# A decode block on one core: the same work, written with waits by hand and a hardware loop for TensorE

## The chip, the core and the metric

The kernel runs on one core of one Trainium2 chip. The metric is the device time of one execution in microseconds. A core has TensorE (PE, with its weight loads listed as PEld), VectorE (DVE), ScalarE (ACT), GpSimd (POOL) and SyncE (SP, which here only issues DMAs), and 16 DMA engines that carry its transfers.

## The reference

Four tokens (B = 4, one position each) go through an attention block over a cache and an MLP, and the results are summed:

```python
x = A_x                                    # (4, 1, 512)
xn = layernorm(x)
q = (xn @ wq) -> (4, 32 heads, 1, 128)
scores = q . k_cache * 128 ** -0.5         # k_cache (4, 32, 4096, 128)
o = softmax(scores) . v_cache              # v_cache (4, 32, 4096, 128)
out = x + o @ wo + B_ref(xn)
# B_ref on one position: xn + gelu(layernorm(xn) @ w3) @ w4, w3 (512, 1792), w4 (1792, 512)
```

All numbers are float32. With one position, the shifts of the mixing step of `B_ref` take only padding, so w1 and w2 have no effect. Both caches are 268 MB each and each byte of them is used once.

## The kernel before, in words

The 128 pairs of batch and head are worked through in 32 groups of four heads (`NJ = 32`, `G = 4`). A group has 8.39 MB of K and as much of V, each as one tile of 128 partitions with 64 KB in a row; 32 partitions belong to a head, and a partition holds 128 positions (`R = 128`).

The scores are not made by TensorE. VectorE multiplies the K tile, in place, by the query, repeated over all partitions of its head and all positions (L219), and sums over the 128 numbers of each position (L220). Then it finds the maximum of each head (L222 to L226: maximum in a partition, a transpose, maximum over the 32). ScalarE takes the exponentials, one head at a time, into `pw`, and keeps their sums in `rs` (L235). TensorE multiplies the weights with V, 32 products a group (L244; each appears as two matmuls and two weight loads in a trace).

The kernel is written in a language with a scheduler: tiles come from pools (`ks` has two buffers for K, `vs` one for V), and the waits follow from what each instruction reads and writes. `tc.issue_after` holds some work back.

Every second group (`y` counts pairs of groups), TensorE's result `pv` is copied by ScalarE (`os`, L250), summed over the partitions of each head by TensorE (`oz`, L253, with the sums of the weights, L255), and divided by VectorE (L257, L260). After eight groups, one batch, `spread` brings the result into the layout `X` that the last product needs (L263 to L266). Every fourth group, `queries` has TensorE spread the queries of four groups over all partitions, into PSUM (`qb`, L209). POOL clears the half of `pw` that the next group doesn't fill (L231).

All large loads are issued by SP, in one order: w3, wq, K(0), K(1), V(0), K(2), V(1), and so on. SP waits for the buffer of the next load to come free: K(j+2) waits for the sums of K(j) (L220), V(j+1) for the products of V(j) (L244). At the end the second buffer of K takes V(31), then w4 goes where V was, and wo follows in five pieces, when the last K tile has been summed (L322).

Before the groups stand two layernorms, the first half of the MLP (L176 to L187) and the queries (`pq`, L198). Behind them stand the second half of the MLP (L284), the product with wo (L331 into `y`, L326 into `total`), a copy (L341) and four small stores (L344).

Of the kernel before, what the change touches and what calls it, by code (L numbers as in the profile page):

```python
# [41 lines left out]
G = 4  # L42


@with_exitstack
def decode_block(ctx: ExitStack, tc: tile.TileContext, x, k, v, wq, wo, w3, w4, out):
# [12 lines left out]
    WC = H * DH // P  # L59

    consts = ctx.enter_context(tc.tile_pool(name="consts", bufs=1))
    ks = ctx.enter_context(tc.tile_pool(name="ks", bufs=2))
    vs = ctx.enter_context(tc.tile_pool(name="vs", bufs=1))
    work = ctx.enter_context(tc.tile_pool(name="work", bufs=2))
    psum = ctx.enter_context(tc.tile_pool(name="psum", bufs=2, space=PSUM))
# [4 lines left out]
    def slot(pool, name):  # L70
        return pool.tile([P, R * DH], F32, tag="rows", name=name)

    def group_rows(flat, j):
        n = G * S * DH
        return flat[j * n:(j + 1) * n].rearrange("(p c d) -> p c d", p=P, c=R)


    w3_slot = slot(vs, "w3")
    w3_sb = w3_slot[:, :NC * F].rearrange("p (c f) -> p c f", c=NC)
    spare = w3_slot[:, NC * F:]  # L80
    xs = spare[:B, :D]
    nc.scalar.dma_start(xs, x.rearrange("b s d -> (b s) d"))
    nc.sync.dma_start(w3_sb, w3.rearrange("(p c) f -> p c f", c=NC))  # L83
    wq_sb = slot(ks, "wq").rearrange("p (c n) -> p c n", c=NC)
    nc.sync.dma_start(wq_sb, wq.rearrange("(p c) n -> p c n", c=NC))  # L85

    K, V = {}, {}

    def load_k(j):
        K[j] = slot(ks, f"k{j}").rearrange("p (c d) -> p c d", c=R)  # L90
        nc.sync.dma_start(K[j], group_rows(kf, j))

    def load_v(j, pool=vs):
        V[j] = slot(pool, f"v{j}").rearrange("p (c d) -> p c d", c=R)
        nc.sync.dma_start(V[j], group_rows(vf, j))

    load_k(0)


    ident = consts.tile([P, P], F32, name="ident")  # L100
    make_identity(nc, ident)
    ones = consts.tile([P, 1], F32, name="ones")
    nc.vector.memset(ones, 1.0)
    eps = consts.tile([B, 1], F32, name="eps")
    nc.vector.memset(eps, EPS)

    sel = consts.tile([P, HP], F32, name="sel")
    nc.vector.reduce_sum(sel, ident.rearrange("p (q m) -> p m q", q=G), axis=AX.X)
    mask = consts.tile([P, G], F32, name="mask")
    nc.vector.reduce_sum(mask, ident.rearrange("p (q m) -> p q m", q=G), axis=AX.X)  # L110

    selb = consts.tile([P, B, G, HP], F32, name="selb")
    for b in range(B):
        nc.vector.tensor_copy(selb[:, b], ident.rearrange("p (q m) -> p q m", q=G)[:, :, b:b + 1].to_broadcast([P, G, HP]))

    pw = consts.tile([P, NG, 32], F32, name="pw")
    os = consts.tile([P, 4, DH], F32, name="os")
    RS = []
    for n in range(2):
        rs = consts.tile([P, 2, G], F32, name=f"rs{n}")  # L120
        nc.gpsimd.memset(rs, 0.0)
        RS.append(rs)
    lt = consts.tile([P, H, 4], F32, name="lt")

    X = consts.tile([P, WC, B], F32, name="X")


    lnc = spare[:B, D:2 * D]
    lnq = os.rearrange("p m d -> p (m d)")[:B, :]

    def layernorm(src, o, name):
        s = work.tile([B, 4], F32, tag="lns", name=f"{name}s")
        nc.vector.reduce_sum(s[:, 0:1], src, axis=AX.X)
        nc.vector.tensor_scalar_mul(s[:, 0:1], s[:, 0:1], 1.0 / D)
        nc.vector.tensor_scalar(lnc, src, s[:, 0:1], None, op0=ALU.subtract)
        nc.vector.tensor_mul(lnq, lnc, lnc)
        nc.vector.reduce_sum(s[:, 1:2], lnq, axis=AX.X)
        nc.scalar.activation(s[:, 2:3], s[:, 1:2], AF.Sqrt, bias=eps, scale=1.0 / D)
        nc.vector.reciprocal(s[:, 3:4], s[:, 2:3])
        nc.vector.tensor_scalar_mul(o, lnc, s[:, 3:4])  # L140

    def transposed(src, o, name):

        nc.gpsimd.memset(o, 0.0)
        pt = psum.tile([P, NC, B], F32, tag="b", name=f"{name}p")
        for c in range(NC):
            nc.tensor.matmul(pt[:, c, :], src.rearrange("b (p c) -> b c p", c=NC)[:, c, :], ident[:B, :B],
                             start=True, stop=True)
        nc.vector.tensor_copy(o[:, :, 0:B], pt)  # L149

    pw_row = pw.rearrange("p g m -> p (g m)")
    xn = pw_row[:B, 0:D]
    x1n = pw_row[:B, D:2 * D]
    layernorm(xs, xn, "xn")
    xnT = X.rearrange("p c b -> p (c b)").rearrange("p (c m) -> p c m", c=NC)
    transposed(xn, xnT, "xnT")
    layernorm(xn, x1n, "x1n")
    x1nT = lt.rearrange("p h q -> p (h q)").rearrange("p (c m) -> p c m", c=NC)
    transposed(x1n, x1nT, "x1nT")


    total = psum.tile([P, P], F32, tag="total", bufs=1, name="total")
    for t in range(4):
        for n, src in enumerate((xs, xn)):
            nc.tensor.matmul(total[32 * t:32 * t + 32, :], ident[:B, 0:32], src[:, P * t:P * t + P],
                             start=(n == 0), stop=False)
    nc.gpsimd.memset(pw, 0.0)


    gT = consts.tile([P, NF, B], F32, name="gT")  # L170

    def mlp_up():
        ph = psum.tile([P, FT], F32, tag="qb", name="ph")
        for c in range(NC):
            for t in range(4):
                nc.tensor.matmul(ph[32 * t:32 * t + 32, :], x1nT[:, c, :], w3_sb[:, c, t * FT:(t + 1) * FT],  # L176
                                 start=(c == 0), stop=(c == NC - 1))
        hs, u, t, gt = (w3_slot[:, n * FT:(n + 1) * FT] for n in range(4))
        nc.scalar.copy(hs.rearrange("p (m i) -> p m i", i=32), ph.rearrange("p (i m) -> p m i", i=32))  # L179
        nc.vector.tensor_mul(u, hs, hs)  # L180
        nc.vector.tensor_scalar(u, u, GELU_B, 1.0, op0=ALU.mult, op1=ALU.add)
        nc.vector.tensor_mul(u, u, hs)
        nc.scalar.activation(t, u, AF.Tanh, scale=GELU_A)
        nc.vector.tensor_scalar(t, t, 1.0, 0.5, op0=ALU.add, op1=ALU.mult)
        nc.vector.tensor_mul(hs, hs, t)
        nc.vector.transpose(gt, hs)
        nc.vector.tensor_copy(gT, gt.rearrange("p (m i) -> p m i", i=32)[:, :, 0:B])  # L187

    mlp_up()


    q_sb = consts.tile([P, 2, 4 * DH], F32, name="q_sb")
    pq = [psum.tile([P, 4 * DH], F32, tag="pv", name=f"pq{n}") for n in range(2)]
    wq_h = wq_sb.rearrange("p c (n j h d) -> p c n h j d", n=2, j=4, h=G)
    for c in range(NC):
        for n in range(2):
            for h in range(G):
                nc.tensor.matmul(pq[n][HP * h:HP * h + HP, :], xnT[:, c, :], wq_h[:, c, n, h],  # L198
                                 start=(c == 0), stop=(c == NC - 1))
    for n in range(2):  # L200
        nc.scalar.mul(q_sb[:, n, :], pq[n], DH ** -0.5)


    QBC, SC, NM, DONE, PVS, OT, SUMMED = {}, {}, {}, {}, {}, {}, {}

    def queries(y):
        b, n = divmod(y, 2)
        QBC[y] = psum.tile([P, 4, DH], F32, tag="qb", name=f"qb{y}")
        nc.tensor.matmul(QBC[y], selb[:, b], q_sb[:, n, :], start=True, stop=True)  # L209

    def scores(j):

        with tc.issue_after(DONE[j - 1]) if j > 0 else nullcontext():
            scores_of(j)

    def scores_of(j):
        SC[j] = work.tile([P, R], F32, tag="sc", name=f"sc{j}")
        q = QBC[j // 4][:, j % 4, :].unsqueeze(1).to_broadcast([P, R, DH])
        nc.vector.tensor_tensor(out=K[j], in0=K[j], in1=q, op=ALU.mult)  # L219
        nc.vector.reduce_sum(SC[j], K[j], axis=AX.X)  # L220
        rm = work.tile([P, 1], F32, tag="rm", name=f"rm{j}")
        nc.vector.reduce_max(rm, SC[j], axis=AX.X)  # L222
        tr = work.tile([P, HP], F32, tag="tr", name=f"tr{j}")
        nc.vector.transpose(tr, rm.to_broadcast([P, HP]))  # L224
        NM[j] = work.tile([P, 1], F32, tag="nm", name=f"nm{j}")
        DONE[j] = nc.vector.tensor_reduce(NM[j], tr, axis=AX.X, op=ALU.max, negate=True).ins  # L226

    def weights(j):
        y, r = divmod(j, 2)
        rs = RS[y % 2]  # L230
        nc.gpsimd.memset(pw[:, :, 16 * (1 - r):16 * (1 - r) + 16], 0.0)  # L231
        for h in range(G):
            s = slice(HP * h, HP * h + HP)
# [4 lines left out]
    def values(j):  # L238
        y, r = divmod(j, 2)
        if r == 0:  # L240
            PVS[y] = psum.tile([P, 4 * DH], F32, tag="pv", name=f"pv{y}")
# [49 lines left out]
    for j in range(NJ):  # L291
# [8 lines left out]
        if j + 2 < NJ:  # L300
            load_k(j + 2)
# [71 lines left out]
```

## Time and profile before

| | us |
|---|---|
| median of three runs | 1308.79 (1308.0 to 1309.28) |
| the profiled execution | 1309.46 |
| its span in the profile | 1307.7 |
| busy: VectorE | 1141.0 (87%) |
| busy: TensorE, weight loads | 356.8, 115.9 |
| busy: ScalarE, POOL | 79.0, 19.1 |
| data moved | 561.38 MB, 429 GB/s over the span |
| instructions in the trace | 5929, of them 2508 matmuls and 2508 weight loads |

The page of the profile lists busy times, DMA queues, the chain that ended last and groups of instructions. A row of a group or of a timeline has the line in the kernel, the engine, the operation, the tile written and the tile read, sizes, and in brackets or behind the bar the idle time ahead of it and what ended that. In a timeline the first two numbers are the start and the length in microseconds from the start of the span. In the list of queues, q1 is SP's, q10 ScalarE's, and the queues named "instruction" carry the engines' own code. A row of windows gives the stretch and its length, each engine's busy time with its count, the granted clock of TensorE, the mean busy share of the 16 DMA engines, and GB/s.

### The profile page before, as it was taken

The page shows a single profiled execution, that of the slowest core. Times are in us where ns is not written, and L with a number is a line of the kernel's source. Part 1 is how long each engine was busy: PE and PEld are TensorE (multiplying, and loading weights), DVE is VectorE, ACT ScalarE, POOL GpSimd, SP SyncE. Part 2 cuts the span into 40 slices and gives each one's busy share as a digit, 9 for nine tenths or more (in the row PEclk, how much of TensorE's full clock was granted, in tenths as well). Part 3 has the DMA queues.
Part 4 walks back from the last instruction along what each step waited for, and adds up shares of the span by engine and source line. Part 5 has one row for each costly group of instructions (what it writes and reads, how often), then busy time and mean ns, then how long its engine had stood idle before and what let it go on. Part 6 is the DMA issues. An engine that isn't in the chain of part 4 may idle for free.

```text
span 1307.7 us, 5929 instructions
## 1 busy us (share of the span) xinstructions
PE 356.8 (27%) x2508; PEld 115.9 (9%) x2508; DVE 1141.0 (87%) x228; ACT 79.0 (6%) x285; POOL 19.1 (1%) x45
## 2 busy tenths in 40 slices
PE   3220323221232321123232033322123332112337
PEld 1000101000010100001010010100001010000102
DVE  3499999998898998888899888898889899888880
ACT  1000000000000000000000000000000000000000
POOL 0000000000000000000000000000000000000000
PEclk8655666656666665666665566665666666566668
DMA  9999999999999999999999999999999999999997
GB/s 403 446 419 439 427 441 425 441 426 439 429 435 432 435 429 435 435 432 435 432 432 439 431 436 429 436 431 434 431 435 436 427 440 427 439 427 438 429 424 317
DMA packets 10434, 561.38 MB, mean 429 GB/s; under 512 B 1172, under 2 KB 1188, under 8 KB 1448
## 3 DMA queue, kind: packets, MB, share of 16 engines
q1 hardware_dynamic: 10384, 561.00, 99.3%
q8 instruction: 19, 0.31, 0.1%
q14 instruction: 7, 0.06, 0.0%
q10 hardware_dynamic: 24, 0.01, 0.0%
HBM read 561.00 MB, written 0.01 MB: 429 GB/s over the span
## 4 chain that ended last, share of the span: by engine, by line
DVE 50%; DMA 49%; issue 0%; SPq 0%; PE 0%; DVEq 0%
DMA k<-in_A_k_cache_dram 46%; DVE sc L220 25%; DVE k L219 25%; DMA wo<-in_A_wo_dram 2%; DVE rm L222 0%; DVE tr L224 0%; PE total L326 0%; SPq L322 0%; DVE nm L226 0%; SPq L85 0%; SPq L83 0%; DVEq L220 0%; DVE ot L260 0%; DVE q_sb L341 0%; DVE rz L257 0%
## 5 line engine op out<-in xcount | busy, mean ns | idle before, releaser
L219 DVE TENSOR_TENSOR k<-k,qb 128x16384 f32<-128x16384 f32 x32 | 551.0, 17220 | 110.5 <-DMA k<-in_A_k_cache_dram 110.5
L220 DVE TENSOR_REDUCE sc<-k 128x128 f32<-128x16384 f32 x32 | 551.0, 17220 | 3.2
L244 PE MATMUL pv<-v,pw 128*32 128x512 f32 x2048 | 294.6, 739 | 897.3 <-DMA v<-in_A_v_cache_dram 897.3
L244 PEld LDWEIGHTS pv<-v,pw 128*32 128x32 f32 x2048 | 80.6, 132 | 1099.1 <-issue 1099.1
L235 ACT ACTIVATE pw<-sc,nm 32x128 f32<-32x128 f32 x128 | 50.9, 398 | 732.8 <-DVE nm L226 730.4
L250 ACT COPY os<-pv 128x512 f32<-128x512 f32 x16 | 9.4, 586 | 437.4 <-PE pv L244 437.4
L231 POOL MEMSET pw<- 128x512 f32 x32 | 16.8, 524 | 1194.1 <-PE pv L244 1194.1
L235 ACT ACTIVATION_READ_ACCUMULATOR pw<-sc,nm 32x1 f32 x128 | 23.5, 184 | 0.0
L253 PE MATMUL oz<-sel,os 128*128 128x8 f32 x128 | 16.2, 253 | 6.8 <-ACT os L250 6.8
L253 PEld LDWEIGHTS oz<-sel,os 128*128 128x128 f32 x128 | 15.8, 191 | 18.6 <-ACT os L250 18.6
L341 DVE COPY q_sb<-total 128x128 f32<-128x128 f32 x1 | 0.3, 292 | 18.5 <-PE total L326 18.5
L257 DVE RECIPROCAL rz<-oz 128x8 f32<-128x8 f32 x16 | 3.2, 198 | 14.3 <-PE oz L255 14.3
L198 PE MATMUL pq<-wq,X 128*32 128x512 f32 x64 | 9.1, 733 | 11.5 <-DMA wq<-in_A_wq_dram 11.5
L222 DVE TENSOR_REDUCE rm<-sc 128x1 f32<-128x128 f32 x32 | 9.2, 286 | 1.1
L209 PE MATMUL qb<-q_sb,selb 128*128 128x512 f32 x16 | 9.0, 644 | 0.0
L331 PE MATMUL y<-wo,X 128*4 128x512 f32 x48 | 7.3, 773 | 5.1 <-DMA wo<-in_A_wo_dram 5.1
L224 DVE STREAM_TRANSPOSE tr<-rm 128x32 f32<-128x32 f32 x32 | 6.8, 211 | 1.1
L265 PE MATMUL xt<-sel,lt 128*128 128x32 f32 x8 | 2.3, 380 | 17.2 <-DVE lt L263 17.2
L226 DVE TENSOR_REDUCE nm<-tr 128x1 f32<-128x32 f32 x32 | 6.0, 186 | 1.1
L255 PE MATMUL oz<-rs,ones 128*128 128x8 f32 x32 | 5.9, 256 | 0.0
L180 DVE TENSOR_TENSOR w<-w 128x448 f32<-128x448 f32 x1 | 0.6, 625 | 5.6 <-ACT w L179 5.6
L176 PE MATMUL ph<-w,lt 128*32 128x448 f32 x32 | 4.9, 780 | 0.3 <-DVE lt L149 0.3
(71 smaller groups left out, 58.3 us busy)
## 6 DMA issues: line engine op xcount, KB each, us to landing
w<-in_B_w_dram SPq DMA_DIRECT2D x2, 3584.0 KB
wo<-in_A_wo_dram SPq DMA_DIRECT2D x1, 4096.0 KB
wo<-in_A_wo_dram SPq DMA_DIRECT2D x1, 2048.0 KB, 28.4
wo<-in_A_wo_dram SPq DMA_DIRECT2D x1, 1024.0 KB, 30.3
wo<-in_A_wo_dram SPq DMA_DIRECT2D x1, 768.0 KB, 31.7
k<-in_A_k_cache_dram SPq DMA_DIRECT2D x32, 42.8
v<-in_A_v_cache_dram SPq DMA_DIRECT2D x32, 29.6
wo<-in_A_wo_dram SPq DMA_DIRECT2D x1, 256.0 KB
```

What stands on the lines that cost most here:

```text
L198: nc.tensor.matmul(pq[n][HP * h:HP * h + HP, :], xnT[:, c, :], wq_h[:, c, n, h], start=(c == 0), stop=(c == NC - 1))
L209: nc.tensor.matmul(QBC[y], selb[:, b], q_sb[:, n, :], start=True, stop=True)
L219: nc.vector.tensor_tensor(out=K[j], in0=K[j], in1=q, op=ALU.mult)
L220: nc.vector.reduce_sum(SC[j], K[j], axis=AX.X)
L222: nc.vector.reduce_max(rm, SC[j], axis=AX.X)
L224: nc.vector.transpose(tr, rm.to_broadcast([P, HP]))
L231: nc.gpsimd.memset(pw[:, :, 16 * (1 - r):16 * (1 - r) + 16], 0.0)
L235: nc.scalar.activation(pw[s, :, c:c + 4], SC[j][s, :].rearrange("p (g w) -> p g w", w=4), AF.Exp, bias=NM[j][s, :], scale=1.0, accum_out=r ...
L244: i = nc.tensor.matmul(PVS[y][32 * t:32 * t + 32, :], pw[:, g, :], V[j][:, 4 * g:4 * g + 4, :], start=(r == 0 and g < 4), stop=(r == 1 and ...
L250: nc.scalar.copy(os, PVS[y].rearrange("p (m d) -> p m d", m=4))
L253: nc.tensor.matmul(oz[:, 0, :], os[:, m, :], sel.rearrange("p (h m) -> p m h", m=4)[:, m], start=(m == 0), stop=(m == 3))
L331: nc.tensor.matmul(y[32 * t:32 * t + B, :], X[:, c, :], wo_sb[:, c], start=False, stop=(c >= CUT - 4))
```

## The change

The whole function is written again with explicit semaphores, inside one section that the scheduler leaves alone (`tc.tile_critical`). `Steps` counts what each engine has done and adds a wait only where the engine has not yet seen that count. The loads, their sizes, their order on SP and what they wait for stay: K(j+2) for the sums of K(j), V(j+1) for the products of V(j). What differs:

- TensorE's work of groups 0 to 30 is one hardware loop (`Fori`) that runs on TensorE alone; its first instruction is asked to be placed at the start of a block of code (`head_slot`). In each turn it waits for V to land (`landed`) and for the weights (`go`), does the 32 products, waits for the copy (`copied`) and sums over partitions. A wait in the loop is followed by a decrement of the semaphore. Group 31 and all that follows it stay straight code.
- The queries are transposed to `qT` once (L255, L257), and for each group VectorE transposes 128 repeated columns into `qb` in SBUF (L267), in place of TensorE's `queries` and PSUM.
- The copy of `pv`, the sums over partitions and the sums of weights are made for each group. ScalarE copies both results to `oz` in SBUF, and VectorE divides once for a batch, in `spread`. TensorE's part of `spread` for batches 0 to 2 comes behind the loop, the copy to `X` once at the end.
- The 16 columns of `pw` that are used are written anew in each group, the others are zero throughout, so POOL's memsets of `pw` go.
- At both ends of the section the engines wait for each other once.

The core of the diff:

```diff
+class Steps:
...
+    def __call__(self, e, make, *after, done=None):
+        self.wait(e, after)
+        i = make(self.engines[e])
+        if done:
+            sem, by, n = done
+            i.then_inc(sem, by)
+            return sem, n
+        self.count[e] += 1
+        i.then_inc(self.sem[e], 1)
+        return self.sem[e], self.count[e]
...
-    def queries(y):
-        b, n = divmod(y, 2)
-        QBC[y] = psum.tile([P, 4, DH], F32, tag="qb", name=f"qb{y}")
-        nc.tensor.matmul(QBC[y], selb[:, b], q_sb[:, n, :], start=True, stop=True)
...
+    with tc.tile_critical():
...
+        for n in range(2):
+            a = do("ACT", lambda e: e.mul(pw_row[:, n * 4 * DH:(n + 1) * 4 * DH], pq[n], DH ** -0.5), pq_ok)
+        d = do("DVE", lambda e: e.transpose(wide, pw_row), a)
+        pw_ok = do("POOL", lambda e: e.memset(pw, 0.0), d)
+        qT_ok = do("DVE", lambda e: e.tensor_copy(qT, wide.rearrange("p (c m) -> p c m", m=32)[:, :, 0:B]), d)
...
+        def queries(j):
+            b, i = divmod(j, ZB)
+            src = qT[:, 4 * i:4 * i + 4, b:b + 1].to_broadcast([P, 4, 32])
+            return do("DVE", lambda e: e.transpose(qb[j % 2].rearrange("p (n m) -> p n m", n=4), src), qT_ok)
+        def scores(j):
...
+            d = do("DVE", lambda e: e.tensor_tensor(out=kt, in0=kt, in1=by, op=ALU.mult), k_in[j], Q[j])
+            SUMMED[j] = do("DVE", lambda e: e.reduce_sum(sc[j % 2], kt, axis=AX.X), d, *PVS[j - 2:j - 1][:j > 1])
...
+        def spread(b):
+            d = do("DVE", lambda e: e.reciprocal(rz, oz[:, b, 1]), COPIED[ZB * b + ZB - 1])
+            d = do("DVE", lambda e: e.tensor_mul(ot, oz[:, b, 0], rz), d)
+            LTS[b] = do("DVE", lambda e: e.tensor_mul(lts[:, b], ot.unsqueeze(2).to_broadcast([P, H, 4]),
+                                                      mask.unsqueeze(1).to_broadcast([P, H, 4])), d)
+        def weights(j):
...
+                free = [PVS[j - 1], OZS[j - 1]] if j else [pw_ok, rs0]
+                do("ACT", make, NMS[j], *free, done=(sems["go"], 1, None) if h == G - 1 else None)
+        def outputs(j):
+            b, i = divmod(j, ZB)
+            do("ACT", lambda e: e.copy(os, pv.rearrange("p (m d) -> p m d", m=4)), PVS[j], done=(sems["copied"], 1, None))
+            COPIED[j] = do("ACT", lambda e: e.copy(oz[:, b, :, 4 * i:4 * i + 4],
+                                                   poz[:, 0:2 * G].rearrange("p (n h) -> p n h", n=2)), OZS[j])
+        k_in[1] = load(ks[1], rows(kf, 1), "k1", 16, pq_ok)
+        load(vs, rows(vf, 0), "landed", None, gT_ok, qT_ok, total_ok)
+        Q = {0: queries(0)}
+        for j in range(NJ):
+            scores(j)
+            if j < LAST:
+                Q[j + 1] = queries(j + 1)
+            if j > 1 and j % ZB == 1:
+                spread(j // ZB - 1)
+            if j + 2 < NJ:
+                k_in[j + 2] = load(ks[j % 2], rows(kf, j + 2), f"k{j % 2}", 16 * (j // 2 + 2), SUMMED[j])
+            weights(j)
+            outputs(j)
+            if j + 1 < LAST:
+                load(vs, rows(vf, j + 1), "landed", None, PVS[j])
+            elif j + 1 == LAST:
+                last_in = load(ks[j % 2], rows(vf, LAST), "last", 16, SUMMED[j])
+                w4_in = load(w4_sb, w4.rearrange("(p m) n -> p m n", m=NF), "w4", 16, PVS[j])
...
+        def values(landed, rows_of):
+            landed()
+            nc.tensor.wait_ge(sems["go"], 1)
+            nc.tensor.sem_inc(sems["go"], -1)
...
+            for g in range(NG):
+                t = g % 4
+                i = nc.tensor.matmul(pv[32 * t:32 * t + 32, :], pw[:, g, :], vt[:, 4 * g:4 * g + 4, :],
+                                     start=(g < 4), stop=(g >= NG - 4))
+            i.then_inc(sems["pv"], 1)
+            nc.tensor.wait_ge(sems["copied"], 1)
+            nc.tensor.sem_inc(sems["copied"], -1)
+            for m in range(4):
+                nc.tensor.matmul(poz[:, 0:G], os[:, m, :], sel.rearrange("p (h m) -> p m h", m=4)[:, m, 0:G],
+                                 start=(m == 0), stop=(m == 3))
+            nc.tensor.matmul(poz[:, G:2 * G], ones.to_broadcast([P, P]), rs, start=True,
+                             stop=True).then_inc(sems["poz"], 1)
...
+        with nc.Fori(0, LAST, engines=OrderedEngineSet([PE]), head_slot={PE: 0}):
+            values(landed, vs)
...
+        values(lambda: do.wait("PE", [last_in]), ks[(LAST - 1) % 2])
...
+        do.wait("SP", [stored])
```

## The prediction

> **What bounds the kernel now.** I read the page first (busy shares, DMA queues, chain), then the chain in order of time, then TensorE's and SP's timelines around one group, the DMA view of short windows, and windows over the last microseconds.
>
> ```profile
> q1 hardware_dynamic: 10384, 561.00, 99.3%
> q8 instruction: 19, 0.31, 0.1%
> q14 instruction: 7, 0.06, 0.0%
> DVE 50%; DMA 49%; issue 0%; SPq 0%; PE 0%; DVEq 0%
> ```
>
> The queue that carries the data is busy 99.3% of the span on 16 engines. VectorE's half of the chain is the other half of one ring: K is fetched again as soon as its sums are done, long before the queue comes to it. So the bytes set the time, and the change leaves all 561.00 MB in the same queue and order. What can move is how evenly the 16 engines finish, the start, and the end.
>
> How evenly: the chain in order of time, K transfers only.
>
> ```profile
> 572.14 42.82 DMA k<-in_A_k_cache_dram
> ...
> 649.56 42.83 DMA k<-in_A_k_cache_dram
> ...
> 726.99 44.36 DMA k<-in_A_k_cache_dram
> ...
> 805.95 42.82 DMA k<-in_A_k_cache_dram
> ```
>
> Landings stand at 614.96, 692.39, 771.35 and 848.77: 77.4 us apart for two groups, but once 78.96. That is a step of 1.54 that is never made good. TensorE's starts on V show another:
>
> ```profile
> 168.51 8.80 PE L244 MATMUL pv<-v,pw 128*32 128x512 f32 x64 [27.28 <-DMA v<-in_A_v_cache_dram]
> 207.21 9.92 PE L244 MATMUL pv<-v,pw 128*32 128x512 f32 x64 [29.91 <-DMA v<-in_A_v_cache_dram]
> 247.40 8.61 PE L244 MATMUL pv<-v,pw 128*32 128x512 f32 x64 [28.23 <-DMA v<-in_A_v_cache_dram]
> ```
>
> 38.70 us, then 40.19: 1.49 late. A group is 16.78 MB, so 38.70 us is 433.5 GB/s. A third is at the end:
>
> ```profile
> 1274.64 8.70 PE L244 MATMUL pv<-v,pw 128*32 128x512 f32 x64 [9.53 <-DMA v<-in_A_v_cache_dram]
> ...
> 1294.37 7.33 PE L331 MATMUL y<-wo,X 128*4 128x512 f32 x48 [5.10 <-DMA wo<-in_A_wo_dram]
> ```
>
> Between these landings lie 3.67 MB of w4 and 4.19 MB of wo: 18.14 us at that rate, but 19.73 pass: 1.59 late. The DMA view has one q8 packet in each of 205 to 248, 725 to 775 and 1270 to 1308 us. It also has one in 650 to 693, where nothing came late. My reading: a fetch of TensorE's code holds up one engine of the 16; a landing waits for the last engine, so only fetches that strike the engine already last show. The last windows (stretch, length, engines, clock, DMA share, GB/s) show how far apart the engines are:
>
> ```profile
> 1297.00:1298.00 1.00, 1.00 (x12) 0.19 (x8) 0.00 (x0) 0.00 (x0) 0.00 (x0) 0.50 0.85 346
> 1299.00:1300.00 1.00, 1.00 (x16) 0.24 (x12) 0.00 (x0) 0.00 (x0) 0.00 (x0) 1.00 0.53 217
> 1301.00:1302.00 1.00, 1.00 (x24) 0.38 (x20) 0.00 (x0) 0.17 (x1) 0.00 (x0) 1.00 0.16 64
> 1303.00:1304.00 1.00, 0.52 (x20) 0.51 (x24) 0.00 (x0) 0.00 (x0) 0.00 (x0) 1.00 0.04 14
> ```
>
> With the windows between (0.70, 0.29, 0.06) the idle share from 1297 to the last landing at 1303.43 adds up to 3.8 us: the average engine is done that long before the last one.
>
> **The change, part by part.** *TensorE's code.* Before, the trace has 2,508 matmuls and as many weight loads; 0.31 MB in 19 packets is 16 KB a packet, one for about 264 of these. Counted from the new code (two passes for each product, as now): 128 before the loop, 74 in it, 230 behind, 432 in all, so 864 with the loads. At 264 a packet the straight code ahead is one packet, the body of 148 with its few waits under one, the code behind under two: 3 to 5 packets, none of them needed between about 50 us and the last group, if a body inside one block is not fetched again. The loop asks to be placed at the start of a block. So the steps at 247 and 771 go: -3.03. The third: a packet is still due when the straight code behind the loop is entered, in the last group, and one in wo. Struck by chance, the last engine loses 1.59 again (price from the third step); else that step goes too. Bounds 0 and -1.59; three such steps in 19 packets make a hit the less likely case, so I take -1.3 (some loss kept for the 7 small packets of q14, of which the new DVE code, a little longer, needs about as many). Sum: -4.3. That is more than the 3.8 above, which can be: the average engine sheds its share of the 19 fetches too.
>
> *What follows in the tail.* wo arrives earlier by 3.0 to 4.6, and the products on it start at the landing. X was ready at 1289.51, 4.9 ahead. Both V(31) and X come 3.0 earlier, X's way gains a copy of poz (0.22 by L266's row) and a few hand-overs, about 0.5, and wo up to 4.6: 2.8 of cover are left. The last blocks wait for the last landing (1303.48), with the sel blocks done at 1302.9, 0.6 ahead; this stays so.
>
> *Waits in TensorE's loop.* V's next load waits for PV, as before. SP issued it at 1225.34, 8.8 after the landing; the K in front of it in the queue landed at 1235.80: 10.4 us of lead. The loop adds two waits with a decrement each ahead of the 32 products, 51 ns each by the trace's semaphore rows: 0.2 us. Cost nothing, cover 10.4; gone, each microsecond over costs 31. Behind a waiting TensorE stand only its own outputs; VectorE needs none of them until the next batch's end.
>
> *ScalarE.* 16 more copies of os (586 ns) and 32 of oz (0.22): 16 us, 0.8 for each group's end. The exponentials now stand behind the copies of the group before: PV ends 1225.3, copy 0.6, products 1.4, copy 0.2: 1227.5, and nm comes at 1232.4: 4.9 of cover, and behind that V, which lands 20 us later.
>
> *VectorE.* 32 transposes of 128 columns: between 211 ns (32 columns) and 645 (448), by the line through both 311: 10 us, less some 6 of reciprocals and products that are now one set for eight groups. Beside it stand 110.5 us of waits for K. The multiplier comes from SBUF instead of PSUM: a product from SBUF of 512 columns takes 680, a reduce 674, and L219 and L220 are equal at 17220: no change, cover 3.4 us a group. Only K(2) is tight: issued 86.25, V(0) landed 90.50. Its chain gains some 0.1 of waits.
>
> *Ahead.* Queries: pq done 40.45, two ScalarE products 1.2, the transpose of 1,024 columns 1.2, copy 0.2, transpose 0.3: 43.4, needed at 51.75. V(0)'s issue moves from 41.04 to about 43 past SP, with K(0) and K(1) in front until 71. POOL loses 32 memsets (16.8 us), all off the path.
>
> *Start and end.* The hand-written section puts one more hand-over between the engines at both ends. At the start the one there is takes 0.3 (POOL from 0.44 to 0.73); SP's first DMA stood at 0.74. Bounds 0 and 0.6; I take +0.2. At the end two waits of SP on the other engines took 0.6 together, between the stores and 1307.7: bounds 0.2 and 0.8; I take +0.4. Neither lies beside anything.
>
> Sum: -4.3 + 0.6 = -3.7. The profiled execution took 1309.46 (span 1307.7, 1.76 around it): 1305.8. The median of the three runs shown, 1308.79, lies 0.67 below it, so the forecast is 1305.1.
>
> **The rivals.** *Third step stays* (25%): -3.03 - 0.2 + 0.6 = -2.6: 1306.2, on the edge of what can be told. A measurement of this kernel can tell about 0.2%, 2.6 us, from no change.
>
> *The fetches are not the cause* (13%): the steps come from memory, nothing goes, and both ends cost 0.6: 1309.4. For it speaks the q8 packet at 650 to 693 without a step; against it that all three steps have one. The Trainium skill ("Runtime: NRT & Kernel Launch", Instruction fetch mechanics) calls the crossing of a 16 KiB block mostly hidden; by that rule nothing would be won here. The steps of 1.49 to 1.59 us speak against it where data fill the queue.
>
> *The loop is fetched again at each turn* (8%), slower: 31 packets and some for 19. Three steps in 19 is one in six: five steps or 7.7 us for 4.6, and 0.6 for the ends: 1308.79 + 3.7 = 1312.5. It decides when the body spans more than is held. Against it stand the body's size, 148 against 264 a packet, and its placing. The same section says that a taken branch whose target isn't held forces a fetch before execution goes on; no trace here has such a branch yet.
>
> *V comes too late* (3%): when a turn adds more than the 10.4 us of lead; 1 us over is +31: 1340.
>
> **How the numbers follow.** Forecast with the third step gone 48%: 1304.5 to 1305.9 (the ends at 0 or at 1.4). Third step stays 25%, half of it faster by over 0.2%. Ends dearer by a microsecond or two 3%: within. Faster 0.48 + 0.13 + 0.01 = 0.62; same 0.12 + 0.02 + 0.13 = 0.27 (no gain, at 1309.4, is within); slower 0.08 + 0.03. The range, 1303.9 to 1309.4, holds all but the two slower rivals and a little below.
>
> **What would show it.** q8 at 3 to 5 packets, none between about 60 and 1240 us; K landings 77.4 apart throughout; the idle share behind the first finished engine under 2.5 us; first DMA of SP near 0.95; the wo products starting about 4 earlier. It is wrong if steps of 1.5 stay without a q8 packet beside them, if q8 counts 31 or more, or if SP's issue of V comes less than 1 us ahead of the K in front.

## The result and the profile after

The changed kernel takes 1306.47 us, the kernel before 1308.70 (medians of 22 runs each): a ratio of 0.9984, 95% interval 0.9977 to 0.9990. That is 2.2 us or 0.17% less: the interval does not hold 1, but the middle falls short of the 0.2% that the prediction set as its bound for faster. In a second set of runs (chip 12) it was 1306.66 against 1308.55, again 0.9984 (0.9975 to 0.9993). The forecast was 1305.1, its range 1303.9 to 1309.4.

The page after, DMA queues and the first groups:

```profile
span 1306.1 us, 6237 instructions
q1 hardware_dynamic: 10384, 561.00, 99.4%
q8 instruction: 4, 0.07, 0.0%
q14 instruction: 6, 0.05, 0.0%
L273 DVE TENSOR_TENSOR ks<-ks,qb 128x16384 f32<-128x16384 f32 x32 | 551.2, 17225 | 88.1 <-DMA ks<-in_A_k_cache_dram 87.6
L267 DVE STREAM_TRANSPOSE qb<-qT 128x128 f32<-128x128 f32 x32 | 9.7, 302 | 0.0
```

The data queue carries the same packets. TensorE's code comes in 4 packets for 19; the other engines' in 6 for 7. VectorE has 87.6 us of waits for K left, so its transposes (302 ns) did find cover.

The chain in order of time, K transfers that carry it, from the same execution:

```profile
648.83 42.87 DMA ks<-in_A_k_cache_dram
726.24 43.57 DMA ks<-in_A_k_cache_dram
804.34 42.87 DMA ks<-in_A_k_cache_dram
...
1191.34 43.56 DMA ks<-in_A_k_cache_dram
```

The step of 1.54 is gone, but two of 0.7 are there, and TensorE's starts on V show a third: 168.82, then 208.20 (39.38 for 38.70). In each of the three intervals stands one packet of q14. The forecast had left 0.3 us for all of these packets together. This profiled execution, 1307.86, is also the slowest of its 22. A profile of the same kernel from the second set (1306.46, the median there being 1306.66) has the same q14 packet between 688 and 695 us, and no step there:

```profile
648.51 42.88 DMA ks<-in_A_k_cache_dram
725.91 42.89 DMA ks<-in_A_k_cache_dram
803.33 42.88 DMA ks<-in_A_k_cache_dram
...
1190.37 43.13 DMA ks<-in_A_k_cache_dram
```

So the same fetch at the same time costs 0.7 in one execution and nothing in another. That is what the forecast's reading asks for, if the two executions differ in which of the 16 engines is last when the groups begin.

The views name no DMA engine, but the packet records of the traces (start, duration, size, queue) show that this is so. A DMA engine starts its next packet some 4 ns before the last one's end, and a tile of K or V ends with one packet of 4 bytes on each of the 16, so the records can be followed engine by engine through the groups. A packet of 16 KB of TensorE's code sets its engine back by 1.55 us, one of 8 KB by 0.65 to 0.98. In the first profile, the three q14 packets of the three steps (at 199.5, 693.7 and 1192.6 us) lie on one engine, and it was the last of all from 110 us on. In the second, the same three lie on an engine that was 1.7 us ahead of the last at 110 us: the first two cost nothing, the third 0.2.

The records also show how the three steps of the kernel before came about. TensorE's packets go round eight of the 16 engines, in the same order each time, so the 3rd, the 11th and the 19th of its 19 (at 211, 760 and 1289 us) struck one engine. It was last from 110 us on, or level with the last. The packet at 683, which made no step, struck an engine that was 1.6 us ahead.

The last windows of the second execution of the changed kernel:

```profile
1298.00:1299.00 1.00, 1.00 (x40) 0.84 (x32) 0.00 (x0) 0.24 (x1) 0.00 (x0) 1.00 0.52 197
1299.00:1300.00 1.00, 0.42 (x19) 0.30 (x16) 0.00 (x0) 0.00 (x0) 0.00 (x0) 1.00 0.08 31
1300.00:1301.00 1.00, 0.76 (x28) 0.38 (x20) 0.17 (x1) 0.00 (x0) 0.00 (x0) 1.00 0.00 0
```

By the packet records the first engine is done with wo 2.6 us ahead of the last, where it was 6.2; the products on the last piece of wo begin at 1299.70, where they began at 1303.48. Summed as in the prediction, the idle share from 1297 on is 1.3 us for 3.8.

### The profile page after: what moved, and what is told of

Its sections match the earlier page's. It is cut to its first block, busy times and chain, and to the rows that moved or that the text cites. A ratio compares the mean times of both kernels' runs of the same rounds, so it can differ in the third digit from the quotient of the medians.

```text
span 1306.1 us, 6237 instructions
## 1 busy us (share of the span) xinstructions
PE 370.4 (28%) x2652; PEld 132.5 (10%) x2652; DVE 1147.7 (88%) x234; ACT 93.0 (7%) x330; POOL 2.4 (0%) x12
## 4 chain that ended last, share of the span: by engine, by line
DVE 51%; DMA 47%; PE 1%; another core or an unknown queue 1%; issue 0%; SPq 0%; ACT 0%; DVEq 0%
DMA ks<-in_A_k_cache_dram 43%; DVE ks L273 25%; DVE sc L275 25%; DMA ks<-in_A_wo_dram 2%; DMA ks<-in_A_wq_dram 2%; PE pv L250 0%; PE pq L250 0%; DVE small L276 0%; DVE qb L267 0%; DVE vs L255 0%; DVE small L277 0%; PE total L148 0%; ACT pw L254 0%; DVE qT L257 0%
## 5 line engine op out<-in xcount | busy, mean ns | idle before, releaser
L273 DVE TENSOR_TENSOR ks<-ks,qb 128x16384 f32<-128x16384 f32 x32 | 551.2, 17225 | 88.1 <-DMA ks<-in_A_k_cache_dram 87.6
L275 DVE TENSOR_REDUCE sc<-ks 128x128 f32<-128x16384 f32 x32 | 551.0, 17220 | 1.1
L336 PE MATMUL pv<-vs,pw 128*32 128x512 f32 x1984 | 288.7, 747 | 872.5 <-PEq L332 872.5
L336 PEld LDWEIGHTS pv<-vs,pw 128*32 128x32 f32 x1984 | 79.4, 134 | 1057.2 <-issue 1057.2
L290 ACT ACTIVATE pw<-sc,small 32x128 f32<-32x128 f32 x128 | 50.9, 398 | 221.9 <-DVE small L278 219.5
L342 PE MATMUL poz<-sel,os 128*128 128x4 f32 x256 | 32.8, 252 | 25.4 <-PEq L340 25.4
L342 PEld LDWEIGHTS poz<-sel,os 128*128 128x128 f32 x256 | 31.0, 191 | 53.5 <-issue 53.5
L290 ACT ACTIVATION_READ_ACCUMULATOR pw<-sc,small 32x1 f32 x128 | 23.5, 184 | 0.0
L255 DVE STREAM_TRANSPOSE vs<-pw 128x1024 f32<-128x1024 f32 x1 | 1.2, 1246 | 17.1 <-ACT pw L254 17.1
L344 PE MATMUL poz<-rs,ones 128*128 128x4 f32 x64 | 11.7, 253 | 0.0
L344 PEld LDWEIGHTS poz<-rs,ones 128*128 128x128 f32 x64 | 9.7, 192 | 0.0
L267 DVE STREAM_TRANSPOSE qb<-qT 128x128 f32<-128x128 f32 x32 | 9.7, 302 | 0.0
```

The source lines that it names most:

```text
L267: return do("DVE", lambda e: e.transpose(qb[j % 2].rearrange("p (n m) -> p n m", n=4), src), qT_ok)
L273: d = do("DVE", lambda e: e.tensor_tensor(out=kt, in0=kt, in1=by, op=ALU.mult), k_in[j], Q[j])
L275: SUMMED[j] = do("DVE", lambda e: e.reduce_sum(sc[j % 2], kt, axis=AX.X), d, *PVS[j - 2:j - 1][:j > 1])
L290: make = lambda e: e.activation(pw[s, :, 4 * h:4 * h + 4], sc[j % 2][s, :].rearrange("p (g w) -> p g w", w=4), AF.Exp, bias=nm[s, :], scal ...
L336: i = nc.tensor.matmul(pv[32 * t:32 * t + 32, :], pw[:, g, :], vt[:, 4 * g:4 * g + 4, :], start=(g < 4), stop=(g >= NG - 4))
L342: nc.tensor.matmul(poz[:, 0:G], os[:, m, :], sel.rearrange("p (h m) -> p m h", m=4)[:, m, 0:G], start=(m == 0), stop=(m == 3))
```

## The experiments

Each run is set against the kernel before on the same chip; where runs on two chips are compared, it is through these ratios, each known to about 0.0009 (1.2 us), so that a difference of two is known to about 1.7 us, or 1.5 with the 22 runs of the changed kernel.

**TensorE's groups as straight code.** One edit to the changed kernel:

```diff
-        with nc.Fori(0, LAST, engines=OrderedEngineSet([PE]), head_slot={PE: 0}):
+        for _ in range(LAST):
             values(landed, vs)
```

> The changed kernel with TensorE's 31 groups written out as straight code again; all else is as changed. Theory (a fetch of code holds up one of 16 DMA engines, and a landing waits for the last engine): q8 goes from 4 packets to about 20, steps of about 1.5 us come back between landings, and the time is some 2.5 us above the changed kernel's 1306.5, at about 1309 (0.7 above if TensorE's fetches never strike the engine that is last now, up to 5 above if they do). Rival (the gain comes from something else in the rewriting, or the steps come from memory): 1306.5, no new steps.

Measured: 1309.48, ratio 1.0007 (0.9998 to 1.0016), 0.23% or 3.0 us above the changed kernel's 0.9984. q8 has 21 packets. The chain shows the steps again:

```profile
494.10 42.90 DMA ks<-in_A_k_cache_dram
571.53 43.80 DMA ks<-in_A_k_cache_dram
...
1036.93 42.87 DMA ks<-in_A_k_cache_dram
1114.33 44.38 DMA ks<-in_A_k_cache_dram
```

The landings are 0.9 and 1.5 us late, with one packet of q8 in each of the two intervals (at 599 and 1108 us). The gain is the loop's: with the code written out, all else in the rewriting brings nothing (1.0007, an interval that holds 1).

**768 instructions more on ScalarE, or on POOL.** They move a spare semaphore up and down, 24 to a group:

```diff
             outputs(j)
+            for n in range(24):
+                nc.scalar.sem_inc(pad, 1 if n % 2 == 0 else -1)
```

On POOL the same lines stand behind a wait for the group's products.

> The changed kernel with 24 instructions a group more on ScalarE that only add to and take from a spare semaphore, 768 in all, behind its copies (about 1.2 us of its 4 us of free time). Theory: q14 gets 6 packets of 8 KB more, and if ScalarE's packets always strike the engine that is last now, each adds a step of 0.7 us: 1306.5 + 4.2 = 1310.7. Rival (small packets are spread over the engines, or hidden): within 0.7 of 1306.5.

> The same 768 instructions on POOL, 24 behind each group's products. Theory: 6 packets of 8 KB more, but of another sequencer; if each sequencer's fetches go to an engine of their own, they strike one that is about 2 us or more ahead of the last, so 4.2 us of steps show as 0 to 2.2: 1306.5 to 1308.7. Rival (any fetch delays a landing, whichever engine it strikes): as much as the padding of ScalarE costs.

Measured: ScalarE 1310.48, ratio 1.0016 (1.0006 to 1.0025), 4.2 us above the changed kernel as forecast; POOL 1308.15, 1.0001 (0.9992 to 1.0010), 2.2 us above it, at the top of what was expected. Both have 12 packets of q14. With ScalarE's padding the chain has step upon step:

```profile
416.00 43.22 DMA ks<-in_A_k_cache_dram
493.76 42.88 DMA ks<-in_A_k_cache_dram
571.16 43.57 DMA ks<-in_A_k_cache_dram
649.26 42.89 DMA ks<-in_A_k_cache_dram
726.68 43.57 DMA ks<-in_A_k_cache_dram
804.77 43.71 DMA ks<-in_A_k_cache_dram
```

The packet records show why. All eight of ScalarE's packets between 100 and 1270 us lie on one engine. It was 1.7 us ahead of the last, so the first two only used up its lead; the third made it the last by 0.4, and each of the five behind that added 0.7. POOL's six lie on another engine, 1.4 us ahead: the third made it the last, and from there on the landings show each one (packets at 571, 802, 998 and 1190 us):

```profile
570.17 43.42 DMA ks<-in_A_k_cache_dram
...
802.94 43.52 DMA ks<-in_A_k_cache_dram
...
958.41 43.53 DMA ks<-in_A_k_cache_dram
...
1191.30 43.58 DMA ks<-in_A_k_cache_dram
```

Two more (164 and 774 us) lie on a third engine. They stand in the same places whatever ScalarE or POOL is given, and change with VectorE's code in the next two experiments, so they are VectorE's. Each of these three thus had its code through one engine of its own, while TensorE's went round eight, and what a fetch costs depends on how far its engine is ahead. That ScalarE's padding cost just what was forecast is in part luck: its engine was not the last, as the forecast took it to be, but the kernel's own ScalarE packets helped to use up its lead.

**ScalarE's work in a loop as well.** Sixteen turns of two groups; VectorE copies the sums, and V's next load waits for the sums over partitions:

```diff
+        with nc.Fori(0, NJ // 2, engines=OrderedEngineSet([ACT])):
+            for j in range(2):
+                weights(j)
+                outputs()
...
-                load(vs, rows(vf, j + 1), "landed", None, PVS[j])
+                load(vs, rows(vf, j + 1), "landed", None, OZS[j])
```

> The changed kernel with ScalarE's work of all 32 groups in a hardware loop too (16 turns of two groups), the copies of the summed results moved to VectorE, and V's next load waiting for the sums over partitions, some 2 us later than now. Theory: ScalarE's three packets of q14, each with a step of 0.7 us, go: 1306.5 - 2.0 = 1304.5, and the landings are even. Rival (the small packets are not what makes those steps): 1306.5. It is wrong and slower if the later issue of V leaves the queue empty.

Measured: 1307.37, ratio 0.9992 (0.9983 to 1.0001). Missed: nothing was won, if not 1 us lost. ScalarE's packets are gone, but VectorE's code had grown by the copies and their waits. Its packets at 164 and 692 us brought its engine to the last place, and a third, between 1232 and 1238, shows in full. TensorE's starts:

```profile
1175.52 9.10 PE L351 MATMUL pv<-vs,pw 128*32 128x512 f32 x64 [26.91 <-PEq L347]
1214.24 8.51 PE L351 MATMUL pv<-vs,pw 128*32 128x512 f32 x64 [27.50 <-PEq L347]
1253.91 9.15 PE L351 MATMUL pv<-vs,pw 128*32 128x512 f32 x64 [29.03 <-PEq L347]
```

38.72, then 39.67: 0.95 late. That explains the profiled execution; whether the median really lies above the changed kernel's was not settled: 1.0 us by the ratios, with 1.5 of uncertainty.

**VectorE's code shorter.** The transpose of the next queries goes ahead of the maxima, so that the product waits for K alone, and the copy of the sums waits for TensorE alone: 59 instructions fewer.

```diff
+            if j < LAST:
+                Q[j + 1] = queries(j + 1)
             d = do("DVE", lambda e: e.reduce_max(rm, sc[j % 2], axis=AX.X), SUMMED[j])
...
-                d = result(j - 1, d)
+                d = result(j - 1)
```

> ScalarE's hardware loop again, and VectorE's code made shorter by 59 instructions: the transpose of the next queries stands ahead of the maxima, so that the product needs no wait of its own for it, and the copy of the results waits for TensorE alone. Theory: with ScalarE's packets gone, VectorE's engine had become the last, by a packet near 1233 us that cost 1.0; with fewer instructions VectorE's third packet falls behind the end, so about 1.0 under the version with ScalarE's loop alone (1307.4) and 1.5 to 2 under the changed kernel of this call. Rival (small packets are not what makes those steps): as the changed kernel.

> The changed kernel as it is, on the chip of this call, so that the versions below can be set against it. Every theory: about 2.2 us under the kernel before.

Measured on one chip: 1306.29 (ratio 0.9982, 0.9973 to 0.9991) beside 1306.66 (0.9984) for the changed kernel. Against the version with ScalarE's loop alone it is 1.3 better by the ratios (1.0 was forecast), a difference between two chips that is not clear of the noise; against the changed kernel 0.4, which can't be told from nothing, where 1.5 to 2 was forecast: a miss. From 339 to 1233 us its chain has no K transfer but those of 42.87 and 42.88. So in a usual run of the changed kernel the small packets cost little, and the 2.1 us of its first profile were bad luck.

**TensorE's code doubled.** 144 spare instructions a group behind the last product of the straight code.

> TensorE's groups as straight code, and 144 instructions a group more on TensorE that only add to and take from a spare semaphore, behind its last product of the group. Theory: q8 goes from 21 packets to about 38; 21 packets left the last engine about 3 steps of 1.5 behind, so 17 more are two to three steps or 3 to 4.5 us more than the straight code alone: 1312.5 to 1314. Rival (fetches are hidden, or the loss of the straight code is TensorE's own): as the straight code, 1309.5.

Measured: 1321.96, ratio 1.0106 (1.0090 to 1.0121), with 38 packets. Only part of it is the packets. The padding took TensorE some 21 us a group (144 instructions at the 51 ns of their rows would be 7), and behind group 30 that no longer had cover:

```profile
1258.76 8.64 PE L337 MATMUL pv<-vs,pw 128*32 128x512 f32 x64 [27.51 <-PEq L333]
...
1290.27 1.46 PE L359 MATMUL pt<-sel,lts 128*128 128x32 f32 x6 [20.83 <-issue]
1291.66 9.25 PE L337 MATMUL pv<-ks,pw 128*32 128x512 f32 x64
```

V(30), ahead of that, began at 1258.76, in the straight code without padding at 1255.74: 3.0 us for 17 packets, the low end of the 3 to 4.5 expected, from one profile of each on two chips. The rest is the padding itself, and the total says nothing on fetches.

**A body across two blocks.** `head_slot={PE: 200}` in place of 0.

> The changed kernel with the loop's head placed at slot 200 of a block of 256, so that the body lies across two blocks. If a turn fetches again what it left (31 or more packets of 16 KB): q8 at 35 to 66, at least five steps of 1.5, 1312 or more, or a stall of TensorE at each turn that the 10 us of lead hide. If both blocks are held: q8 at 4 to 6 and the time of the changed kernel.

Measured: 1306.62, ratio 0.9984 (0.9975 to 0.9993), q8 4 packets: the changed kernel's time. The second packet comes at 96.9 us, inside the first turn (its products begin at 90.93), where the changed kernel had it at 47.5, so the body does run on into a second block. A turn fetches nothing again, and the placing of the loop brought nothing.

**The first group in two halves**, on top of the version with both loops:

```diff
+                for n in range(2):
+                    part = slice(n * H0, n * H0 + H0)
...
+                    SUMMED[0] = do("DVE", lambda e: e.reduce_sum(sc[0][:, part], kt[:, part], axis=AX.X), d)
+                    k_in[2] = load(ks[0][:, n * H0 * DH:(n + 1) * H0 * DH], rows(kf, 2)[:, n * H0 * DH:(n + 1) * H0 * DH], "k0", 32 + 16 * n, SUMMED[0])
```

> The version with ScalarE's loop and VectorE's shorter code, and the first group's product and sums made in two halves, so that the first half of K(2) is asked for some 17 us earlier, while K(1) and V(0) are still in the queue. Theory: the last engine's lead over the others is set near 88 us, where K(2) comes to a queue that is about to run empty; with K(2) there in time the landings from then on come 0.4 to 1.3 us earlier, and with them the end: 1305.0 to 1305.9, where the version without the halves is at 1306.3. Rival (the start is spread by the two early fetches of TensorE's code alone): less than 0.3 gained.

> The version with ScalarE's loop and VectorE's shorter code once more, beside the one with the halves on the same chip: 1306.3.

Measured: 1305.61 (ratio 0.9976, 0.9967 to 0.9985) beside 1306.25 (0.9982): 0.6 better, inside the 0.4 to 1.3 expected. The two intervals overlap, but they share the noise of the kernel before; set beside each other on the one chip, ten of the 11 runs lie below the fastest of the other version's 11. TensorE's first starts, without and with the halves:

```profile
90.91 9.21 PE L351 MATMUL pv<-vs,pw 128*32 128x512 f32 x64 [49.52 <-PEq L347]
130.33 5.35 PE L351 MATMUL pv<-vs,pw 128*32 128x512 f32 x24 [28.08 <-PEq L347]
```

```profile
90.92 9.92 PE L359 MATMUL pv<-vs,pw 128*32 128x512 f32 x64 [50.52 <-PEq L355]
129.70 5.87 PE L359 MATMUL pv<-vs,pw 128*32 128x512 f32 x32 [26.74 <-PEq L355]
```

39.42 and 38.78 from V(0) to V(1), 38.70 being the queue's own pace. K(2) had been issued at 86.46, when V(0), landed at 90.9, was the last thing in the queue; now its first half goes at 69.41. This version is 3.2 us under the kernel before and the best of all that ran.

## Why the prediction was right, and by how much it was off

*What bounds the kernel, and what moves.* Right. The bytes and the pace stayed (38.70 us a group), and all that was won was the last engine's delay. The straight code (+3.0) and ScalarE's padding (+4.2) show that code fetches make it, and the packet records show them on the last engine.

*The packets.* Forecast 3 to 5, measured 4. The two steps at 247 and 771 went as forecast. The third went too: in the second profile the products on wo begin at 1290.56 for 1294.37, 3.8 earlier; "about 4" was forecast. That the third went was taken for chance, with three steps in 19 packets as its odds. It isn't chance which engine is struck: with eight engines in turn, each gets two or three of 19 packets, and the three steps were one engine's share. What was luck is where the few packets left fell. The one at 1279 us in the second profile struck an engine 2.7 us ahead of the last, the one at 1280 in the first an engine 4.0 ahead.

*The sum* was -4.3 for the steps and +0.6 for the ends, from one profiled execution to another. By the second profile the copy of `total` moved from 1304.60 to 1300.83, 3.77 earlier, though the start is 0.21 later: 3.98 of steps, 0.3 less than forecast. The small packets were put among "some loss kept", at some 0.3 in all; they cost 0.25 in that execution, as allowed. What it lacks was lost ahead of the steps: V(2) came 0.71 later than before, of which the start explains 0.21, and the sum had no term for the rest. In the first profile V(2) was 0.31 later and the small packets cost 2.1: there that term was mis-sized, and the profiled execution was only 1.6 under that of before.

*The ends.* The start was +0.21 (SP's first DMA at 0.95 for 0.74), forecast +0.2. From the copy to the end of the span it was 3.10 and is 3.87: +0.77, where +0.4 was taken and 0.8 was the bound. The section's own end waits for the stores and then for all engines, and the end of the kernel does so once more.

*The step to the median* was off too. The profiled execution of before stood 0.67 above the median, and that difference was taken off the forecast as if it were the same for both kernels. It is no constant: in 22 runs before's median is 0.76 under its profiled execution, while the changed kernel's profiles lie 1.4 above their median (the first) and 0.2 below (the second). That the steps themselves make the difference fits, but was not shown. Counted by the second profile, 0.3 + 0.4 + 0.67 are the 1.4 between 1305.1 and 1306.47. With them the gain falls from 3.7 to 2.3; before's own median, 0.1 lower in 22 runs than in three, makes it 2.2, which is under 0.2%: by the prediction's own bound that is "same", which it gave 0.27, and not "faster", which it gave 0.62.

*The covers* held. V's next load was issued at 1224.89 with K landing at 1234.93: 10.0 us of lead for 10.4. V(0) was issued at 44.10 for the 43 forecast, with K(0) and K(1) still ahead of it.

*The rivals.* That memory made the steps is ruled out by the straight code; a loop fetched again at each turn by q8's 4 packets, with the body in one block and across two. The Trainium skill's rule ("Runtime: NRT & Kernel Launch", Instruction fetch mechanics) that the crossing of a 16 KiB block is mostly hidden holds for the engine that runs the code: TensorE shows no gap over 0.4 us between the products of a group, and a group's products take 8.4 to 9.9 us with a fetch among them, 8.5 to 10.0 without (the kernel before and the straight code). It doesn't hold for the data beside it: 1.5 us at each that strikes the last engine. What the section says of a taken branch out of what is held, no run here shows.

## What to carry to other kernels

Where the data queue is full from end to end, code is traffic too: TensorE's straight code, in 21 packets of 16 KB for 4, cost 3.0 us of 1309, since each fetch holds up one engine of 16 by 1.55 us and a landing waits for the last. A mean busy share of 99% can't show it; look for landings that are late once and never make it good, and at how the DMA share runs out at the end. Before a profiled execution is moved to the median by a constant, ask whether the difference is made of the very thing that the change removes.

## What the runs showed of the hardware that I had not expected

- A packet of 8 KB set its engine back by 0.65 us (POOL's), 0.69 (ScalarE's) or up to 0.98 (VectorE's), near half of one of 16 KB (1.55).
- TensorE's code came through eight DMA engines in turn, every eighth packet through the same one; the code of ScalarE, VectorE and POOL each through one engine throughout, three different ones.
- The order of the engines is there when the groups begin: in the changed kernel's two traces, engines that no fetch struck kept their places to 0.2 us from 110 us to the last V. But it was another order in each, so the same q14 packet near 692 us cost 0.7 in one execution and nothing in the next.
- Increments of a semaphore by TensorE, one behind the other, began some 150 ns apart (144 of them filled 20.8 us), though each one's row is 51 ns, as long as that of a satisfied wait.
